# Attention through induced points and a two-layer network in one kernel: some steps of the first attention put at other visits, and a planner that links a late chain's parts and scores the last visit

## The chip, the cores and the metric

The kernel runs on one core of one Trainium2 chip. The metric is the device time of one execution in microseconds (us); of several executions the median is taken. A core has five engines that work side by side, each with its own instructions in order: TensorE (PE in the profile) multiplies matrices into PSUM, of which the kernel uses 8 banks of 128 x 512 fp32 numbers; ScalarE (ACT) computes functions such as exponentials and ReLUs and copies; VectorE (DVE) does element-wise work and reductions; GpSimd (POOL) does element-wise work on SBUF; SyncE (SP) issues DMAs here. An engine that needs another's result waits for a semaphore.

## The reference

Four batches of 12480 rows of 128 numbers pass two attentions and then a network with a parametric ReLU. Cut to what matters:

```python
def mab(q, kv):
    s = scale * (q @ kv.transpose(0, 2, 1))
    a = np.exp(s - s.max(-1, keepdims=True))
    a /= a.sum(-1, keepdims=True) + 1e-09
    return a @ kv
h = mab(I, x)          # 32 induced points look at all rows of a batch
x = mab(x, h)          # each row looks at the 32 results
h = x @ w_in           # 128 -> 2048
g = np.maximum(h, 0.0) + alpha * np.minimum(h, 0.0)
out = g @ w_out        # 2048 -> 128
```

## The kernel before

**Folding.** A row's second attention is a product of its 32 weights (`a2`) with the 32 results of its batch, and `w_in` follows at once; so the kernel forms `HW` = results x `w_in` once a batch, and a row's hidden numbers are its weights times `HW`. The parametric ReLU is split in two: alpha times the hidden number, which is linear and goes through `HA` (32 x 128) in `linear`, and (1 - alpha) times a plain ReLU, with 1 - alpha inside `W1`.

**Visits.** The loop at the end runs over blocks of 512 rows, four visits a block (`visits`), 390 visits in all; the last two blocks, made of rows that are left over, take 4 and 2. In a visit TensorE computes four banks `hh` of hidden numbers (`visit`, L848), then the second product of the visit before (`second`, L874, 16 products that add up in the bank `bp`). Between the two, each of the four `hh` is turned into a bf16 tile `gt` by a ReLU, on ScalarE (L861) or VectorE (L863). Each fourth visit a block's sum is copied out of PSUM and stored (`finish`, L927 or L929, store L934), and every eighth visit two blocks' linear parts are computed (L901).

**Steps between the visits.** What prepares later blocks is put behind a visit's products by hand: `at(n, fn, ...)` files a step under visit n (`todo`), and the loop runs a visit's steps in the order in which they were filed. There are two kinds.

- For each group of 2048 rows (16 visits, first visit n): the second scores (`b_scores`) are copied out of PSUM, their maximum is taken (`b_max`, VectorE), subtracted (`b_less_pool`, GpSimd), the exponential taken (`b_exp`, ScalarE, the step that stands as a lambda), summed (`b_sum`, GpSimd), inverted (`b_rec`, VectorE), multiplied into four copies (`b_mul`, GpSimd) and transposed by a DMA (`b_turn`) into `a2`. The list `when` gives their visits.
- For each piece of the next batch (six of 2048 rows with eight visits between them, and a short one of 192 rows, number 1): load, cast (GpSimd), a transposing DMA (`a_turn`), scores against the induced points with their running minimum (`a_scores_least`, at the visit `score`), exponential (`a_exp`, ScalarE, at `look`), the factor that rescales older sums (`a_fac`, ScalarE), a transposing DMA of the exponentials (`a_e1`, one visit behind `look`), and the product with the rows, added up (`a_h_add`, at `join`). At a batch's end `a_max`, `a_factors`, `a_parts`, `a_den` and `a_sum` close the sums and `a_w_both` and `a_lin` form `HW` and `HA`.

All DMAs of this phase are issued by SP, in the order of the program.

**The planner.** Before the loop records anything, `Plan.choose` searches over all visits with a beam of 64 states. For each visit it chooses which of the four ReLUs go to ScalarE ("a") and VectorE ("v"), which engine copies an output, and for each step's chain of work (its `cost`, a list of engine and ns) whether it runs at once ("n") or late ("l"), that is behind the second ReLU of the next visit (`run_waiting`). `Plan.step` advances modelled times of TensorE, ScalarE, VectorE and the PSUM banks for one visit. A state's score is TensorE's modelled time plus a part of what the other engines lag behind. The best path decides the engines, the order and the banks of the built kernel; nothing is decided while it runs.

Of the kernel before, what the change touches and what calls it, by code (L numbers as in the profile page):

```python
# [30 lines left out]
def kernel(  # L31
# [82 lines left out]
    class Plan:  # L114
# [41 lines left out]
        def step(self, state, n, relus, ways):  # L156


            pe, a, v, e1, free, held, late = state
            cols, linear, accs, last, chains = self.visits[n]  # L160
            busy = {"a": a, "v": v}
            free, held, used = list(free), dict(held), []

            def take(pe):
                k = min(range(BANKS), key=lambda k: max(free[k] + self.SEM, pe))
                used.append(k)
                pe = max(pe, free[k] + self.SEM)
                free[k] = self.NEVER
                return pe, k

            hh, mine = [], []
            for r in range(R):
                k = min(range(BANKS), key=lambda k: free[k])
                used.append(k)
                mine.append(k)
                pe = max(pe, free[k] + self.SEM) + 4
                free[k] = self.NEVER
                hh.append(pe + cols * 0.417 + self.ARRIVE)
            out = []
            for r in range(R):  # L180
                if r == 2:
                    for k, ns, ready, bank in late:
                        busy[k] = max(busy[k], ready) + ns
                        if bank is not None:
                            free[bank] = busy[k] + 100
                lat, per, over = self.RELU[relus[r]]
                out.append(max(busy[relus[r]], hh[r]) + lat + per * cols)
                free[mine[r]] = out[r]
                busy[relus[r]] = out[r] - over
            pe += cols * 0.417  # L190
            for k in accs[0]:
                if k not in held:
                    pe, held[k] = take(pe)
            pe += linear + self.MODE
            for k in accs[1]:
                if k not in held:
                    pe, held[k] = take(pe)
            for r in range(R):
                pe = max(pe, e1[r] + self.SEM) + last * self.FREE
            waits = []  # L200
            for chain, way in zip(chains, ways):
                ready, bank = 0, None
                for kind, ns in chain:
                    if kind == "!":
                        continue
                    if kind == "free":
                        free[ns] = ready + 100
                        continue
                    if kind == "acc":
                        ready, bank = pe + self.ARRIVE, held.pop(ns)  # L210
                        continue
                    if kind in "ps":
                        if kind == "s":
                            pe, bank = take(pe)
                        pe += ns
                        ready = pe + self.ARRIVE
                        continue
                    k = way[0] if kind == "f" else kind
                    ns = self.COPY[k] if kind == "f" else ns
                    if way[-1:] == "l":  # L220
                        waits.append((k, ns, ready, bank))
                    else:
                        busy[k] = ready = max(busy[k], ready) + ns
                        if bank is not None:
                            free[bank] = ready + 100
                    bank = None
                if bank is not None:
                    free[bank] = ready + 600
            new = pe + self.MODE, busy["a"], busy["v"], tuple(out), tuple(free)
            return (*new, tuple(held.items()), tuple(waits)), used  # L230

        def choose(self):
            start = tuple(430.0 if k == BANKS - 1 else 0.0 for k in range(BANKS))
            beam = [((0.0, 0.0, 330.0, (0.0,) * R, start, (), ()), None)]
            relus = ["".join(w) for w in product("av", repeat=R) if 0 < w.count("a") < R]
            for n, (*_, chains) in enumerate(self.visits):
                ways = []
                for chain in chains:
                    kinds = [k for k, _ in chain]
                    if "f" in kinds:  # L240
                        ways.append([e + w for e in "av" for w in "nl"])
                    elif "!" in kinds or not {"a", "v"} & set(kinds):
                        ways.append([""])
                    else:
                        ways.append(["n", "l"])
                found = {}
                for state, path in beam:
                    for way in product(*ways):
                        for relu in relus:
                            new, used = self.step(state, n, relu, way)  # L250
                            at = new[0] + 390
                            over = max(new[1] - at, 0) + max(new[2] - at, 0)
                            over += sum(w[1] for w in new[6]) * 0.3
                            score = new[0] + 0.3 * over
                            ends = sorted(max(x - new[0], -200) for x in new[4])
                            key = (
                                *(int(x - new[0]) // 16 for x in new[1:3] + new[3]),
                                *(int(x) // 16 for x in ends if x < self.NEVER / 2),
                                new[6],
                            )  # L260
                            if key not in found or score < found[key][0]:
                                found[key] = (score, new, (path, relu + "".join(way), used))
                best = sorted(found.values(), key=lambda f: f[0])[: self.WIDTH]
                beam = [(new, path) for _, new, path in best]
            path, taken, banks = beam[0][1], [], []
            while path:
                path, these, used = path
                taken.append(these)
                banks.append(used)
            self.taken = iter("".join(reversed(taken)))  # L270
            self.banks = iter([k for used in reversed(banks) for k in used])

    plan = Plan()
# [972 lines left out]
    def at(n, fn, *args, cost=()):  # L1246


        todo.setdefault(max(n, 0), []).append((fn, args, cost))
# [11 lines left out]

    for b, s, nt in groups[1:]:
        n = first[b, s]
        when = [n - 23, n - 19, n - 16, n - 14, n - 13, n - 11, n - 9, n - 6]
        if (b, s) == (0, 1):
            when = [0, 2, 3, 6, 7, 9, 9, 9]
        if (b, s) == (0, 2):
# [32 lines left out]
    for b in range(B - 1):  # L1300
# [3 lines left out]
        for p, pc in enumerate(whole_pieces):  # L1304
            m = n + (8 * (p - 1 + (not b and p > 2)) if p > 1 else p)
            load, cast, turn = m - 3, m + 6, m + 8
            score = m + 15 if p > 1 else n + 16
            look = score + 1 + (p == 1)
            join = m + (24 if p == whole_pieces[-1].k else 23) if p > 1 else n + (31 if p else 23)
            if not b:  # L1310
                load, cast, turn = {
                    0: (-1, -1, 6), 1: (-1, 9, 10), 2: (4, 9, 11)
                }.get(p, (load, cast, turn))
                score, look = (score, look) if p > 1 else (score + 4, look + 4)
                join = n + 31 if p < 2 else n + 39 if p < 3 else join
            f = pc.full
            if load >= 0:
                at(load, on, b + 1, a_load, pc)
# [12 lines left out]
                cost=[("s", 215 if f else 85), ("v", 800 if f else 460)],  # L1331
            )
            at(look, on, b + 1, a_exp, pc, cost=[("a", 717 if f else 430)])
            at(look + 2, on, b + 1, a_fac, pc, cost=[("a", 220)] if p else [])
            at(look + 1, on, b + 1, a_e1, pc)
            small_at(
                join, on, b + 1, a_h_add, pc, cost=[("s", 226 if f else 115), ("v", 260)]
# [13 lines left out]
    for n, (blk, i) in enumerate(visits):  # L1351
        before = visits[n - 1][0] if n else None
        nt = before.nt * before.per if n else 0
        chains = [cost for _, _, cost in todo.get(n, ()) if cost]
        if i == 0 and n > NV:
            copy = ("f", 0) if n > ST else ("v", 610)
            chains.insert(0, [("acc", before.k), copy])
            if n == 2 * NV:
                chains.insert(0, [("acc", 0), copy])
        both = [b.k for b in pairs.get(n, ())]  # L1360
        cost = nt * Plan.FREE if both else 0
        plan.visits.append(
            (blk.nt * blk.per * P, cost, (both, [before.k] if n else []), nt, chains)
        )
    plan.choose()

    prev = None
# [49 lines left out]
```

## Time and profile before

| | |
|---|---|
| median of 3 runs | 591.48 us (591.35 to 591.55) |
| the profiled execution | 593.02 us |
| its span, first to last instruction | 591.1 us, granted clock 1.0 |
| DMA, packets' time as a share of 16 engines, main queue | 56.0% |
| VectorE, ReLUs (L863) | 706 of 683 ns mean |
| a load of 1 MB (`xs`), issue to landing, median | 6.4 us |
| transposing DMA of a piece (`xT`), median | 6.6 us |
| transposing DMA of a group's weights (`a`), median | 4.7 us |
| transposing DMA of exponentials (`e`), median | 3.0 us |

The profile is of one execution, taken by the hardware profiler. "L874" is line 874 of the kernel. A group's row gives its line, engine, operation, tiles (written <- read), shapes and count, then the busy time in us and the mean ns of one, then the idle time of the engine just before. The chain of waits follows the work that ended last back from the last instruction; its pieces are listed as start, length, engine, tile and line. The timeline lists start, length, engine, line, operation, tiles and count; a bracket tells how long the engine had stood before and what ended it. For a DMA the length in SP's timeline is that of its issue; the time to landing stands in the DMA view.

### The profile page before, as it was taken

To read this page: it belongs to the slowest core of one execution; us is meant where nothing else is said; L and a number is where in the kernel's file an instruction comes from. 1 tells how busy PE (TensorE), PEld (TensorE's weight loads), DVE (VectorE), ACT (ScalarE), POOL (GpSimd) and SP (SyncE) were. 2 spreads that over 40 slices of the span, in tenths; PEclk is the share of its full clock that TensorE was granted. 3 is DMA by queue.
4 is the path that set the end of the run, shared out by engine and by line. 5 is a ranking of instruction groups with operands and counts; after the bars stand their busy time and mean duration, and the time that the engine had idled before them with its cause. 6 is when DMAs were issued, how large, how long until landed. Compare 5 with 4: busy or idle time off the path is not lost.

```text
span 591.1 us, 23015 instructions
## 1 busy us (share of the span) xinstructions
PE 580.7 (98%) x9443; PEld 436.2 (74%) x9443; DVE 534.4 (90%) x974; ACT 536.8 (91%) x1085; POOL 217.2 (37%) x259
## 2 busy tenths in 40 slices
PE   7899999999999999999999999999999999999997
PEld 3577777777777777777777777777777777777776
DVE  5799999988998998999999899999999999999996
ACT  5699999999999999999998999999999998999986
POOL 3575552523325426313226256124034134144110
PEclk9999999999999999999999999999999999999999
DMA  8786799734188899432256999741331331441321
GB/s 334 252 213 169 153 256 217 116 91 74 38 240 185 184 205 222 103 82 70 77 151 176 216 216 221 143 99 38 92 75 54 91 81 48 118 85 58 91 69 48
DMA packets 121964, 80.56 MB, mean 136 GB/s; under 512 B 103761, under 2 KB 105729, under 8 KB 118785
## 3 DMA queue, kind: packets, MB, share of 16 engines
q1 hardware_dynamic: 121632, 78.99, 56.0%
q8 instruction: 74, 1.21, 0.8%
q14 instruction: 34, 0.27, 0.1%
q10 hardware_dynamic: 224, 0.09, 0.1%
HBM read 28.07 MB, written 25.56 MB: 91 GB/s over the span
## 4 chain that ended last, share of the span: by engine, by line
PE 94%; DMA 3%; POOL 1%; DVE 0%; ACT 0%; issue 0%; DVEq 0%; SPq 0%; POOLq 0%
PE bp L874 66%; PE hh L848 22%; DMA xs<-in_x_dram 3%; PE bp L901 2%; PE hh L684 2%; PE hh L498 1%; PE hh L378 1%; POOL xn L348 0%; PE bp L1000 0%; PE hh L638 0%; DVEq L1412 0%; PE hh L607 0%; PE hh L622 0%; PE hh L1033 0%; PE hh L819 0%
## 5 line engine op out<-in xcount | busy, mean ns | idle before, releaser
L861 ACT ACTIVATE gt<-hh 128x512 bf16<-128x512 f32 x854 | 455.2, 606 | 34.3 <-PE hh L848 29.4
L863 DVE TENSOR_SCALAR gt<-hh 128x512 bf16<-128x512 f32 x706 | 453.4, 683 | 24.5 <-PE hh L848 13.2
L874 PE MATMUL bp<-W,gt 128*128 128x128 bf16 x6240 | 417.2, 220 | 0.7 <-DVE gt L863 0.7
L874 PEld LDWEIGHTS <-gt 128*128 128x128 bf16 x6240 | 349.3, 98 | 85.0 <-issue 76.5
L848 PE MATMUL hh<-a,HW 32*128 32x512 bf16 (+2 forms) x1664 | 156.0, 370 | 0.5 <-DVE a L827 0.5
L798 POOL TENSOR_TENSOR rep<-e,rc 128x2048 bf16<-128x2048 f32 (+2 forms) x26 | 84.8, 3265 | 23.0 <-DVE rc L789 22.6
L766 POOL TENSOR_TENSOR e<-e,smx 128x512 f32<-128x512 f32 (+1 forms) x24 | 24.6, 1027 | 154.6 <-ACT gt L861 79.4
L848 PEld LDWEIGHTS <-HW 32*128 32x128 bf16 x1664 | 40.4, 91 | 42.0 <-issue 5.9
L752 POOL TENSOR_TENSOR t<-e 128x256 f32<-128x256 f32 (+1 forms) x24 | 17.2, 718 | 144.1 <-ACT e L728 144.1
L927 ACT COPY ob<-bp 128x512 f32<-128x512 f32 (+1 forms) x63 | 36.9, 586 | 4.6 <-PE bp L874 1.7
L752 POOL TENSOR_TENSOR t<-t 128x128 f32<-128x128 f32 (+3 forms) x100 | 30.5, 305 | 7.8
L331 POOL CAST xn<-xs 128x2048 bf16<-128x2048 f32 x17 | 32.1, 1891 | 1.3 <-DMA xs<-in_x_dram 0.7
L929 DVE COPY ob<-bp 128x512 f32<-128x512 f32 x31 | 21.2, 684 | 5.2 <-PE bp L874 5.2
L417 DVE TENSOR_SCALAR_CACHE_REDUCE s<-hh 128x512 f32<-128x512 f32 (+2 forms) x29 | 17.9, 619 | 2.2 <-PE hh L378 1.9
L901 PEld LDWEIGHTS <-a 32*128 32x128 bf16 x392 | 14.9, 93 | 5.8 <-issue 0.2
L901 PE MATMUL bp<-HA,a 32*128 32x128 bf16 x392 | 19.1, 214 | 0.0
L443 ACT ACTIVATE e1T<-s,rm 128x512 bf16<-128x512 f32 (+1 forms) x25 | 17.9, 718 | 1.1 <-DVE rm L427 1.0
L761 DVE TENSOR_REDUCE smx<-e 128x16 f32<-128x512 f32 (+1 forms) x24 | 15.9, 661 | 0.0
L728 ACT ACTIVATE e<-e 128x512 f32<-128x512 f32 (+1 forms) x24 | 15.0, 624 | 0.0
L742 ACT COPY e<-hh 128x512 f32<-128x512 f32 (+1 forms) x22 | 13.4, 610 | 0.0
L684 PE MATMUL hh<-hT,xT 128*128 128x32 bf16 x372 | 13.0, 176 | 0.0
L523 DVE SCALAR_TENSOR_TENSOR hs<-hs,fac,hh 128x128 f32<-128x128 f32 (+1 forms) x21 | 7.2, 344 | 6.0 <-PE hh L498 5.3
(117 smaller groups left out, 195.2 us busy)
## 6 DMA issues: line engine op xcount, KB each, us to landing
out_dram<-ob SPq DMA_DIRECT2D x97, 256.0 KB, 2.5
xs<-in_x_dram SPq DMA_DIRECT2D x23, 1024.0 KB, 6.4
xs<-in_x_dram SPq DMA_DIRECT2D x2, 512.0 KB, 8.4
w_in_f<-in_moe_w_in_dram SPq DMA_DIRECT2D x1, 1024.0 KB, 9.9
a<-rep SPq DMA_TRANSPOSE x27, 4.7
xs_left<-in_x_dram SPq DMA_DIRECT2D x4, 96.0 KB, 5.8
xT<-xn SPq DMA_TRANSPOSE x18, 6.6
e<-e1T SPq DMA_TRANSPOSE x18, 3.0
```

What stands on the lines that cost most here:

```text
L331: nc.gpsimd.tensor_copy(out=st.xn[s][:], in_=xs[:])
L684: nc.tensor.matmul(ps[w, t, :], st.xT[:, tile0[s] + t, w], hTs[b][:], start=True, stop=True)
L752: nc.gpsimd.tensor_tensor(out=t[:, :n], in0=src[:, :n, :w], in1=src[:, :n, w : 2 * w], op=ADD)
L766: nc.gpsimd.tensor_tensor(out=st.e2[s][:, :n], in0=st.e2[s][:, :n], in1=st.m2[s][:, :n].unsqueeze(2).broadcast_to([P, n, M]), op=SUB,)
L798: nc.gpsimd.tensor_tensor(out=st.rep[s][:, ts], in0=st.e2[s][:, ts].unsqueeze(2).broadcast_to([P, n, R, M]), in1=rc[:, ts].unsqueeze(2).un ...
L848: nc.tensor.matmul(hh[:, q * cols + w.start : q * cols + w.stop], HWs[b][rows, v * P : (v + 1) * P], a2[rows, t0 : t0 + nt, :].rearrange(" ...
L861: nc.scalar.activation(out=gt[:, :cols], in_=hh[:, :cols], func=RELU)
L863: nc.vector.tensor_relu(gt[:, :cols], hh[:, :cols])
L874: nc.tensor.matmul(blk.acc[:, t * C : (t + 1) * C], gt[:, (q * nt + t) * P : (q * nt + t + 1) * P], W1[:, k, :], start=(not blk.begun), st ...
L901: nc.tensor.matmul(blk.acc[w, t * C : (t + 1) * C], blk.a2[rows, blk.t0 + t, w], HAs[b][rows, :], start=(not blk.begun and t == 0), stop=F ...
L927: nc.scalar.copy(out=ob[:, :nt], in_=acc)
L929: nc.vector.tensor_copy(out=ob[:, :nt], in_=acc)
```

## The change

Four things are changed; no instruction is added or removed.

```diff
             for r in range(R):
                 if r == 2:
-                    for k, ns, ready, bank in late:
-                        busy[k] = max(busy[k], ready) + ns
+                    done = 0
+                    for k, ns, ready, bank, linked in late:
+                        done = max(busy[k], ready, done if linked else 0) + ns
+                        busy[k] = done
                         if bank is not None:
                             free[bank] = busy[k] + 100
...
-                ready, bank = 0, None
+                ready, bank, linked = 0, None, False
...
                     if way[-1:] == "l":
-                        waits.append((k, ns, ready, bank))
+                        waits.append((k, ns, ready, bank, linked))
+                        linked = True
...
                             score = new[0] + 0.3 * over
+                            if n == len(self.visits) - 1:
+                                score = new[0] - self.MODE
+                                for ready in new[3]:
+                                    score = max(score, ready + self.SEM) + self.end * self.FREE
...
-        when = [n - 23, n - 19, n - 16, n - 14, n - 13, n - 11, n - 9, n - 6]
+        when = [n - 23, n - 20, n - 16, n - 13, n - 12, n - 10, n - 9, n - 6]
...
             score = m + 15 if p > 1 else n + 16
-            look = score + 1 + (p == 1)
+            look = score + 3 + 3 * (p == 1)
...
+            if p == 1 and b:
+                score, look = score + 4, look + 4
...
-            at(look + 2, on, b + 1, a_fac, pc, cost=[("a", 220)] if p else [])
+            at(look + 3, on, b + 1, a_fac, pc, cost=[("a", 220)] if p else [])
             at(look + 1, on, b + 1, a_e1, pc)
...
+    plan.end = visits[-1][0].nt * visits[-1][0].per
     plan.choose()
```

- In the planner's model a late chain's second part now begins only when its first part is done; before, the parts of a late chain could overlap.
- In the last visit a state is scored by the modelled end of the last second product, which waits for each ReLU in turn, instead of the end of the visit.
- In each group but the first two the maximum is filed one visit earlier, and the exponential, the sum and the reciprocal one visit later each.
- A whole piece's exponential is filed two visits later, the short piece's four visits later against its scores, and these scores, from batch 2 on, four visits later themselves. The transposing DMA of the exponentials moves with the exponential, the factor by one visit more. The products that use them stay where they were.

The planner's choices follow from these: the engines of ReLUs and copies and what is late change from visit 12 on.

## The prediction

> **What bounds the kernel now.** First the page: its busy shares and its chain of waits.
>
> ```profile
> span 591.1 us, 23015 instructions
> PE 580.7 (98%) x9443; PEld 436.2 (74%) x9443; DVE 534.4 (90%) x974; ACT 536.8 (91%) x1085; POOL 217.2 (37%) x259
> PE bp L874 66%; PE hh L848 22%; DMA xs<-in_x_dram 3%; PE bp L901 2%; PE hh L684 2%; PE hh L498 1%; PE hh L378 1%; POOL xn L348 0%; PE bp L1000 0%; PE hh L638 0%; DVEq L1412 0%; PE hh L607 0%; PE hh L622 0%; PE hh L1033 0%; PE hh L819 0%
> ```
>
> TensorE is the bound, and the change takes no matmul from it. So the only thing to win is time in which TensorE stands. To find that time I read the chain of waits piece by piece. An undisturbed visit is two pieces, 0.33 us for the first products and 1.00 us for the second; a longer piece holds a wait.
>
> ```profile
> 403.64 0.33 PE hh L848 x4
> 403.97 1.00 PE bp L874 x16
> ```
>
> From visit 0 (30.5 us) to the end of the full blocks (577 us) I find 27 such pieces, and one wait that shows itself as other engines' work. Each excess below is the row less 0.33 or 1.00.
>
> ```profile
> 30.51 0.40 PE hh L848 x4
> ...
> 101.60 0.45 PE hh L848 x4
> ...
> 196.50 0.55 PE hh L848 x4
> ...
> 241.17 0.46 PE hh L848 x4
> ...
> 378.85 0.46 PE hh L848 x4
> ```
>
> By stretch the excesses add up to 0.74 us up to 130 us (batch 1 is being prepared), 1.29 us from 164 to 263 us (batch 2), 0.70 us from 302 to 401 us (batch 3), and none that counts in the visits between, which prepare nothing. The largest wait stands by itself; the first fence is the chain, the second the timeline of TensorE's weight loads where it ends:
>
> ```profile
> 131.63 0.59 ACT gt L861
> 132.22 0.20 ACT ex L577
> ...
> 132.44 0.18 DVE dx L587
> ...
> 132.80 0.61 DVE gt L863
> ```
>
> ```profile
> 133.45 0.45 PEld L874 LDWEIGHTS <-gt 128*128 128x128 bf16 x8 [0.67 <-DVE gt L863]
> ```
>
> Here `a_parts` of batch 1 was put off (a late chain) into a visit where ScalarE has three ReLUs. VectorE reaches `dx`, which needs ScalarE's `ex`, and stands; the ReLU behind `dx` comes late, and TensorE's second product with it. 0.67 us is lost. One more wait, 0.37 us, stands in the very last second product:
>
> ```profile
> 585.05 1.29 DVE L863 TENSOR_SCALAR gt<-hh 128x512 bf16<-128x512 f32 x2 [0.43 <-PE hh L848]
> 585.10 1.09 ACT L861 ACTIVATE gt<-hh 128x512 bf16<-128x512 f32 x2
> 586.39 0.67 PEld L874 LDWEIGHTS <-gt 128*128 128x128 bf16 x12 [0.37 <-DVE gt L863]
> ```
>
> All that can be won is 0.74 + 0.67 + 1.29 + 0.70 + 0.37 = 3.8 us, or 0.6%.
>
> **The linked chain** (planner). The two parts of `a_parts`, and those of `a_factors`, are now costed one after the other. In the changed plan `a_parts` of batch 1 is still late, in visit 69, but the ReLUs of that visit go to VectorE first and ScalarE last, so nothing on VectorE stands behind `dx` in that visit, and ScalarE has no ReLU of the visit ahead of `ex`, only one copy (0.59 us, below). I take the 0.67 us as won. The least is 0.4 us: the copy's 0.59 us may still push ScalarE's two ReLUs back by the part of it that exceeds the 0.3 us or so a visit leaves ScalarE over.
>
> **Exponentials two visits later, short piece apart.** What the change spreads is seen where a piece's scores are taken:
>
> ```profile
> 238.62 0.68 DVE L417 TENSOR_SCALAR_CACHE_REDUCE s<-hh 128x512 f32<-128x512 f32 x1
> 239.42 3.07 DVE L863 TENSOR_SCALAR gt<-hh 128x512 bf16<-128x512 f32 x5
> 239.90 0.72 ACT L443 ACTIVATE e1T<-s,rm 128x512 bf16<-128x512 f32 x1
> ```
>
> VectorE spends 0.8 us on the scores (238.62 to 239.42), and at once ScalarE spends 0.72 us on the exponential. VectorE then runs five ReLUs without a pause, and the next first product but one waits 0.13 us (241.17 above). The waits at 101.6 and 378.9 us have the same place, and others too: one to three visits behind scores. In the changed plan ScalarE takes three ReLUs in the visit after the scores, and VectorE more of them where the exponential stands. The wait at 196.5 us and its like in batch 3 follow the visit where the whole and the short piece are scored together; now they are four visits apart. So the cause of most of the 0.74 + 1.29 + 0.70 us goes. Up to visit 11 the plan is the same and keeps its 0.15 us. I take 2/3 of the rest, 1.7 us, as won, before what follows; ends: 0 and 2.6 us.
>
> **What the moved step issues.** Each exponential is followed by a transposing DMA of `e1`, also two visits later, while the product that needs it (`a_h`, L498) stays. On SP's queue it is moved past an output's store, and, for every other whole piece, past `b_turn`, the transposing DMA of a group's weights. SP takes its instructions in order, and landings in the trace follow that order. The fourth piece of batch 2, in the timeline of SP:
>
> ```profile
> 225.86 4.10 SPq L355 DMA_TRANSPOSE xT<-xn  x1
> 230.42 1.71 SPq L474 DMA_TRANSPOSE e<-e1T  x1
> 232.23 0.53 SPq L934 DMA_DIRECT2D out_dram<-ob  x1
> 232.86 2.33 SPq L806 DMA_TRANSPOSE a<-rep  x1
> ```
>
> The DMA view restricted to this `e1` and this `b_turn` gives issue to landing, and TensorE's timeline the product's start:
>
> ```profile
> e<-e1T SPq DMA_TRANSPOSE x1, 3.9
> a<-rep SPq DMA_TRANSPOSE x1, 5.8
> 237.90 0.29 PE L498 MATMUL hh<-xn,e 128*32 128x128 bf16 x8
> ```
>
> Before, `e1` landed at 230.42 + 3.9 = 234.3, 3.6 us ahead of its product, and `b_turn` at 238.7. Behind `b_turn` it lands some 0.5 us after that (it moves a quarter of what `b_turn` moves, and that takes 2.33 us to issue), 239.2: 1.3 us late if `b_turn` stays where it is. But `b_turn` no longer has `e1` (1.71 us of issue) ahead of it. The group's exponential is one visit later, its GpSimd sum with it, and the piece's cast stands behind that sum, so `a_turn` (225.86) and `b_mul`, which forms the weights, move back by up to one visit, 1.33 us; `a_turn` then ends its issue near 231.3, and `b_turn` can follow a store behind it, near 231.5 to 231.9. That is 1.0 to 1.4 us earlier than now, and `e1` lands from 237.8 to 238.2: at its product, not before. So I cost it at 0 to 0.3 us against the old clock, but TensorE cannot come earlier than that here: what batch 2 had won up to this product is given back, about half of its 1.29 us. In batch 3 the same rows are earlier:
>
> ```profile
> 370.50 2.65 SPq L806 DMA_TRANSPOSE a<-rep  x1
> a<-rep SPq DMA_TRANSPOSE x1, 4.6
> 375.58 0.41 PE L498 MATMUL hh<-xn,e 128*32 128x128 bf16 x16
> ```
>
> 370.5 + 4.6 + 0.5 = 375.6 with `b_turn` unmoved, and 1 us less with it earlier: no wait there. I take 0.6 us as given back in all.
>
> The Trainium skill bears on this in DMA: Bandwidth & Descriptors, section "Latency and other measured facts": a transposing DMA moves 261 GB/s. By that the 128x2048 bf16 of `b_turn` (0.52 MB) would take an estimated 2.0 us instead of the 5.8 us from issue to landing seen here; `e1` behind it would land near 234, and nothing would be given back: 0.6 us less, still inside the forecast's own range. The trace speaks against it.
>
> **Group steps by one visit.** The group's maximum one visit earlier, its exponential, sum and reciprocal one later; `b_mul` and `b_turn` stay. GpSimd is busy 37% and covers it; if it didn't, the first products of the next group would wait for `b_turn`, which in batch 3 lands at 375.1, in visit 238 of a group whose first visit is 240, so more than a visit is spare. Cost 0.
>
> **Engines.** Comparing the programs' orders, 8 ReLUs go from ScalarE to VectorE, and 12 output copies the other way.
>
> ```profile
> L861 ACT ACTIVATE gt<-hh 128x512 bf16<-128x512 f32 x854 | 455.2, 606 | 34.3 <-PE hh L848 29.4
> L927 ACT COPY ob<-bp 128x512 f32<-128x512 f32 (+1 forms) x63 | 36.9, 586 | 4.6 <-PE bp L874 1.7
> ```
>
> ScalarE gets 12 x 0.586 - 8 x 0.533 (455.2/854) = 2.8 us more, VectorE about as much less. At 91% and 90% busy both lie under TensorE on the whole. In quiet visits the group's exponential and an output copy now stand in neighbouring visits of ScalarE, twelve times in the plan; I cost this at 0, since ScalarE is a visit ahead there, and keep up to 0.13 us each (one exponential, one copy and six ReLUs at 0.52 us are 4.3 us, the three visits 4.2 us), 1.6 us.
>
> **The last visit** is now scored to its end: ScalarE first, VectorE second. The second ReLU then ends at 585.10 + 1.09 = 586.19 instead of 585.05 + 1.29 = 586.34: 0.15 us won; ends 0 and 0.37.
>
> **The sum.** 0.67 + 1.7 - 0.6 + 0.15 = 1.9 us won. The profiled execution took 593.02 us, its span 591.1 and 1.9 around it, 1.5 us above the median of the runs (591.48); it becomes 591.1. The median becomes 591.48 - 1.9 = 589.6 us. Its own range goes from 0.9 us won (0.4, half of the 1.1 us that the exponentials keep, nothing at the end) to 3.6 us (0.67 + 2.6 + 0.37, nothing given back): 587.9 to 590.6.
>
> **The rivals.** *The win is eaten.* TensorE gets no faster than its DMAs: everything won ahead of an `e1` product is given back there, and only what comes behind the last such product of a batch stays: the 0.67 us, 0.13 us twice or so, the end's 0.15 us, about 1.0 us; 590.5 us, and with small new waits 591. For it: the landings above; against it: batches 1 and 3 have room.
>
> *Slower: `e1` behind `b_turn`.* If `b_turn` does not move forward, `e1` lands late at the seven places (two or three a batch) where it follows on SP with four visits to its product. The price of each lies between 0.06 us (375.64 against 375.58) and 1.3 us (batch 2); at the middle, 0.7, seven cost 4.9 us, less the 1.0 us that stays won: +3.9 us, 595.4 us. It decides once `b_turn` of batch 2's fourth piece is issued later than some 231.9 us on the old clock. Against it: the room that `e1` leaves ahead of `b_turn`. The Trainium skill has the rule behind it in the same page, section "Queues, rings and completion order": each DMA engine consumes a ring's descriptors in ring order. The order of the landings agrees.
>
> *The plan's costs do not hold.* The new plan loses in quiet visits (1.6 us) about what it wins elsewhere: 591.2 us. Against it: the old plan, made with the same costs, has no wait there.
>
> **How the numbers follow.** Forecast 0.57, win eaten 0.18, slower 0.13, costs do not hold 0.12. 0.2% is 1.2 us, about what counts as a change. Faster by more than that (below 590.3): nine tenths of the forecast, a third of the eaten win and some of the last, 0.60. Slower (above 592.7): 0.13 and a part of the last, 0.16. Within: 0.24. The range goes from 587.9 to 592.4; outside remain the slower case and little else.
>
> **What would show it.** Right: no chain through `dx` near 132 us; no excess one to three visits behind scores; the last second product resumes near 586.2 less what was won. The `e1` step is wrong if L498 waits for a DMA; the chain then has a DMA piece `e<-e1T`, and `b_turn` lands just ahead. The quiet-visit cost is wrong if L848 or L874 pieces between 263 and 302 us, or beyond 401 us, exceed 0.33 and 1.00. The prediction falls if such waits add up to more than 0.7 us.

## The result, and the profile after

The changed kernel takes 593.16 us (median of 22 runs, 591.92 to 595.20), the kernel before 591.48 us (22 runs, 591.25 to 592.26). The ratio is 1.0028, 95% interval 1.0020 to 1.0035: slower by 1.7 us, where 1.9 us less was forecast. The runs also spread over 3.3 us, against 1.0 us before.

The profiled execution took 592.05 us, one of the shorter ones. Its page:

```profile
span 590.3 us, 22988 instructions
PE 579.8 (98%) x9443; PEld 436.3 (74%) x9443; DVE 532.8 (90%) x969; ACT 537.1 (91%) x1090; POOL 216.7 (37%) x259
PE bp L881 65%; PE hh L855 21%; PE bp L908 2%; DMA e<-e1T 2%; PE hh L691 2%; PE hh L505 1%; PE hh L385 1%; DMA xs<-in_x_dram 1%; PE hh L370 1%; PE bp L1007 1%; PE hh L488 0%; PE hh L645 0%; ACT gt L868 0%; PE hh L614 0%; PE hh L629 0%
```

Lines have moved by seven (L874 is now L881, L848 L855, L498 L505). The span is shorter than the 591.1 us of before, and that misleads. In the chain of waits the first visit begins here:

```profile
29.18 0.40 PE hh L855 x4
```

In the profile of before it began at 30.51, though both programs are the same up to there; in every later profile of these runs it lies between 28.4 and 29.3 us. The profiled execution of before had lost 1.3 us on its way to the first visit. From the first visit to the end it took 591.1 - 30.5 = 560.6 us; the changed kernel takes 590.3 - 29.2 = 561.1.

New in the chain is a DMA, `e<-e1T`. Who waits for it stands in the waits of TensorE's weight loads from 29 to 590 us (waiting instruction, releaser, us in total, times, longest):

```profile
PEld L505 <- DMA e<-e1T: 1.7, 3, 1.1
PEld L505 <- DMA e<-e1T_left: 1.2, 1, 1.2
```

Before there was no such row. 2.9 us in four waits, and the timeline of the weight loads has the places, visits 126, 142 and 222:

```profile
212.42 0.11 PEld L505 LDWEIGHTS <-e 128*32 128x32 bf16 x2 [1.18 <-DMA e<-e1T_left]
212.84 0.23 PEld L505 LDWEIGHTS <-e 128*32 128x32 bf16 x16 [0.31 <-DMA e<-e1T]
...
236.29 0.23 PEld L505 LDWEIGHTS <-e 128*32 128x32 bf16 x16 [0.31 <-DMA e<-e1T]
...
351.40 0.23 PEld L505 LDWEIGHTS <-e 128*32 128x32 bf16 x16 [1.11 <-DMA e<-e1T]
```

The two long ones are where the short and the second whole piece of batches 2 and 3 are joined. SP's timeline ahead of the first, and the DMA view of the three transposes in it:

```profile
205.95 2.33 SPq L813 DMA_TRANSPOSE a<-rep  x1
208.37 1.34 SPq L481 DMA_TRANSPOSE e<-e1T_left  x1
209.76 1.75 SPq L481 DMA_TRANSPOSE e<-e1T  x1
```

```profile
a<-rep SPq DMA_TRANSPOSE x1, 6.1
e<-e1T_left SPq DMA_TRANSPOSE x1, 4.0
e<-e1T SPq DMA_TRANSPOSE x1, 3.0
```

`b_turn` lands at 205.95 + 6.1 = 212.1, the two `e1` right behind it at 212.4 and 212.8, and at these times L505 starts. SP spends 5.4 us on issuing the three. The chain shows the stop from TensorE's side: its products end at 209.1, and nothing of TensorE stands in it until 212.84.

```profile
208.75 0.36 PE hh L855 x4
209.12 0.59 ACT gt L868
209.71 0.05 issue
209.76 3.03 DMA e<-e1T
212.79 0.04 issue
212.84 0.41 PE hh L505 x16
```

(A chain names who released whom; TensorE itself worked on up to 211.4 us there and then stood for 1.0 us.)

### The profile page after: what moved, and what is told of

Same layout as the page of the kernel before. It is cut to its first block, busy times and chain, and to the rows that moved or that the text cites. A ratio compares the mean times of both kernels' runs of the same rounds, so it can differ in the third digit from the quotient of the medians.

```text
span 590.3 us, 22988 instructions
## 1 busy us (share of the span) xinstructions
PE 579.8 (98%) x9443; PEld 436.3 (74%) x9443; DVE 532.8 (90%) x969; ACT 537.1 (91%) x1090; POOL 216.7 (37%) x259
## 4 chain that ended last, share of the span: by engine, by line
PE 95%; DMA 3%; ACT 1%; DVE 0%; issue 0%; POOL 0%; SPq 0%; POOLq 0%
PE bp L881 65%; PE hh L855 21%; PE bp L908 2%; DMA e<-e1T 2%; PE hh L691 2%; PE hh L505 1%; PE hh L385 1%; DMA xs<-in_x_dram 1%; PE hh L370 1%; PE bp L1007 1%; PE hh L488 0%; PE hh L645 0%; ACT gt L868 0%; PE hh L614 0%; PE hh L629 0%
## 5 line engine op out<-in xcount | busy, mean ns | idle before, releaser
L870 DVE TENSOR_SCALAR gt<-hh 128x512 bf16<-128x512 f32 x714 | 458.7, 685 | 29.9 <-PE hh L855 18.2
L881 PE MATMUL bp<-W,gt 128*128 128x128 bf16 x6240 | 416.5, 220 | 0.0
L881 PEld LDWEIGHTS <-gt 128*128 128x128 bf16 x6240 | 349.4, 98 | 82.6 <-issue 74.1
L855 PE MATMUL hh<-a,HW 32*128 32x512 bf16 (+2 forms) x1664 | 154.5, 371 | 0.5 <-DVE a L834 0.5
L855 PEld LDWEIGHTS <-HW 32*128 32x128 bf16 x1664 | 40.2, 91 | 41.8 <-issue 5.8
L934 ACT COPY ob<-bp 128x512 f32<-128x512 f32 (+1 forms) x75 | 44.7, 596 | 1.0 <-PE bp L881 0.5
L936 DVE COPY ob<-bp 128x512 f32<-128x512 f32 x19 | 13.0, 684 | 0.0
```

What stands on the lines that cost most here:

```text
L855: nc.tensor.matmul(hh[:, q * cols + w.start : q * cols + w.stop], HWs[b][rows, v * P : (v + 1) * P], a2[rows, t0 : t0 + nt, :].rearrange(" ...
L870: nc.vector.tensor_relu(gt[:, :cols], hh[:, :cols])
L881: nc.tensor.matmul(blk.acc[:, t * C : (t + 1) * C], gt[:, (q * nt + t) * P : (q * nt + t + 1) * P], W1[:, k, :], start=(not blk.begun), st ...
L934: nc.scalar.copy(out=ob[:, :nt], in_=acc)
```

## The experiments

Two theories. **Q**: the loss is the queue: `e1` is issued behind `b_turn` and lands after its product could start. **P**: the planner's new engines, order and lateness cost the time.

### e1 ahead of b_turn, the plan unchanged

```diff
-        when = [n - 23, n - 20, n - 16, n - 13, n - 12, n - 10, n - 9, n - 6]
+        when = [n - 23, n - 20, n - 16, n - 13, n - 12, n - 10, n - 9, n - 5]
```

> The changed kernel, only b_turn filed one visit later, so that SP issues the e1 transposes ahead of it; b_turn has no cost in the planner, so the plan is the same. Theory Q (the loss is e1 landing late behind b_turn on SP's queue): the waits before L505 at visits 126, 142 and 222 (1.08 + 0.35, 0.20, 1.15 us in the changed kernel's profile) go, the time falls from 593.2 to about 590.3 us (589.6 to 591.0), and the spread of its runs from 3.3 us to about 1 us. Should b_turn then land after its group's first visit, L855 at visits 128 and 224 waits instead. Theory P (the new plan's engines and lateness cost the time): no change, 592.5 to 593.8 us.

590.24 us (589.34 to 591.78), ratio to before 0.9980, 0.9971 to 0.9989. Moving one step on SP's queue by one visit (`b_turn`, one DMA a group), with the same plan, takes 2.9 us from the changed kernel. The waits at 126, 142 and 222 are gone. The spread is 2.4 us, not 1: the profiled execution, the longest of the runs (591.78), has other late landings, and the one that the expectation named for `b_turn` at visit 128:

```profile
PEld L505 <- DMA e<-e1T: 2.0, 2, 1.1
PEld L855 <- DMA a<-rep: 0.7, 1, 0.7
```

The loss stays away although the plan is the same, so P is refuted as its cause; Q stands. But it doesn't cover every late `e1`: the two left in this profile are at visits 214 and 230, and no `b_turn` is issued just ahead of them.

### One part alone

Each is the kernel before with one part of the change's diff, and nothing else.

> The kernel before with the planner's two changes alone (linked late chains, last visit scored to its end). Q: the 0.67 us wait behind dx goes and some 0.15 us at the end, 590.7 us (590.3 to 591.3). P: the planner's choices are what loses, 592 us or more.

> The kernel before with the pieces' steps alone moved (exponentials, e1 transposes, factors, the short piece's scores). Q: the late e1 at visits 126 and 222 are there, waits of 1 us or more before L498, 592.5 us (591.8 to 594) and a spread of 2 us or more. P: no such waits, 590 to 591.3 us.

> The kernel before with the group steps alone moved (maximum one visit earlier; exponential, sum and reciprocal one later). Q: nothing on TensorE's path, 591.5 us (591.1 to 592). P: output copies and group exponentials stand in neighbouring visits, L848 or L874 pieces over 0.33 and 1.00 us between 263 and 302 us, 592.5 us or more.

| alone on the kernel before | median, us | runs from to | ratio to before, 95% |
|---|---|---|---|
| planner | 590.14 | 589.81 to 591.01 | 0.9972 to 0.9989 |
| pieces' steps | 593.27 | 592.41 to 595.09 | 1.0022 to 1.0051 |
| group steps | 593.91 | 593.65 to 594.28 | 1.0031 to 1.0056 |

The planner's part wins 1.2 us by itself, a little more than Q's range allowed; its profile has no wait behind `dx` and none for a DMA. The pieces' steps bring the late `e1` with them, more of it than the changed kernel's profile shows, in a longer execution (594.77 us); the waits of the weight loads:

```profile
PEld L498 <- DMA e<-e1T: 2.4, 3, 1.3
PEld L498 <- DMA e<-e1T_left: 1.3, 1, 1.3
```

These 3.7 us are not all that this execution lost there. TensorE's timeline at visit 126 and, behind it, the granted clock in stretches of 1 us (from and to, length, TensorE's busy time and matmuls, granted clock as a share of full speed, busy share and GB/s of the DMA engines):

```profile
212.69 0.29 PE L498 MATMUL hh<-xn_left,e 128*32 128x128 bf16 x2 [1.14 <-DMA e<-e1T_left]
214.12 0.41 PE L498 MATMUL hh<-xn,e 128*32 128x128 bf16 x16 [1.15 <-DMA e<-e1T]
...
215.01 1.50 PE L874 MATMUL bp<-W,gt 128*128 128x128 bf16 x16
...
216.98 1.89 PE L874 MATMUL bp<-W,gt 128*128 128x128 bf16 x16
```

```profile
215.00:216.00 1.00, 1.00 (x18) 0.73 0.60 213
216.00:217.00 1.00, 1.00 (x10) 0.50 1.04 369
217.00:218.00 1.00, 1.00 (x14) 0.50 0.96 313
218.00:219.00 1.00, 1.00 (x13) 0.56 0.96 335
```

Right behind two stops of 1.14 and 1.15 us the granted clock fell to half for about 3 us, and the second products took 1.50 and 1.89 us instead of the 1.07 us that this view gives an undisturbed one. From the drop in these four rows (0.27 + 0.50 + 0.50 + 0.44) that is an estimated 1.7 us at most on top of the waits. No other profile here has such a drop while TensorE works, also not those with single stops of 1.0 to 1.6 us or with two of 0.96 and 0.79 us.

The group steps lose 2.6 us alone, where Q had expected nothing, though not in the quiet visits that P had named. The wait behind `dx` of batch 1 now stands in all three batches, here in batch 2 (chain):

```profile
257.66 0.59 ACT gt L861
258.25 0.19 ACT ex L577
...
258.47 0.18 DVE dx L587
...
258.83 0.61 DVE gt L863
```

And at visit 126 VectorE has its hands full: sums, scores, running minimum, then two ReLUs, for the last of which TensorE waits 0.22 us. That place alone explains little, as the kernel before waits 0.17 us for VectorE in the same second product.

### Two parts, and the short piece

The first two take one part out of the changed kernel; the third leaves the short piece's exponential nearer to its scores:

```diff
             if p == 1 and b:
-                score, look = score + 4, look + 4
+                score, look = score + 4, look + 1
```

> The changed kernel with the pieces' steps put back (planner and group steps changed). Alone the group steps lost 2.6 us, with a wait behind dx in all three batches. If the unlinked model was the reason, the linked one takes these waits away: 590.2 us (589.5 to 590.8), no wait before L505. If the group steps cost by themselves (a copy and an exponential in neighbouring visits of ScalarE): 591.5 to 593 us.

> The changed kernel with the group steps put back (planner and pieces' steps changed). Q: e1 is as late as in the changed kernel, waits of 1 us or more before L505 at visits 126 and 222, 592.5 us (591.6 to 593.5), spread 2 us or more. P: 589.5 to 590.5 us, if the group steps were what cost the time.

> The changed kernel with the short piece's exponential three visits earlier in batches 2 and 3, so that at visits 122 and 218 one e1 instead of two stands behind b_turn. Q: the second piece's e1 is issued 1.2 to 1.3 us earlier but still lands behind b_turn; the wait at visit 126 falls from 1.4 to some 1.0 us, at 222 from 1.15 to some 0.3 us; 592.3 us (591.5 to 593). If the pair were the whole cause: both waits gone, 590.3 us.

Planner and group steps: 591.58 us (ratio 0.9993 to 1.0011). The waits behind `dx` are gone, so the unlinked model was one reason for them; but 1.4 us over the planner alone stay. In its profile 0.5 us of that lie between visits 24 and 92 and 0.5 us between 92 and 160, as short waits at many places, the longest two at these first products (0.33 us undisturbed):

```profile
131.09 0.67 PE hh L855 x4
...
176.67 0.57 PE hh L855 x4
```

Why the moved group steps bring them isn't shown. Both guesses were half right. Planner and pieces' steps: 593.04 us (1.0022 to 1.0045), with 1.8 + 1.1 us of waits for `e1` in its profile: putting the group steps back changes nothing as long as `e1` is late. The short piece early: 590.71 us (589.80 to 591.85, ratio 0.9981 to 0.9997), better than expected of Q. The wait at 222 is gone and the stretch of batch 3 short; at 126 there is one wait still, for the second piece's `e1` alone:

```profile
PEld L505 <- DMA e<-e1T: 1.6, 1, 1.6
```

In the medians one `e1` fewer behind `b_turn` takes back 2.4 us of the changed kernel's loss, but the profile doesn't show so much. Batch 3 (visits 188 to 256) takes 98.1 us instead of 99.2; batch 2 (visits 92 to 160) takes 99.6 us as against 99.7, since its one wait is no shorter than the two of the changed kernel together (1.18 + 0.31). So the pair decides at visit 222; at 126 the order behind `b_turn` is enough. What else the medians gain is open.

### All exponentials one visit earlier

```diff
-            look = score + 3 + 3 * (p == 1)
+            look = score + 2 + 3 * (p == 1)
```

> The changed kernel with every exponential, and its e1 transpose, one visit earlier (two visits behind the scores instead of three; the short piece's too), so that SP issues e1 a visit ahead of b_turn, and b_turn stays where it is. Theory Q (queue order): no wait before L505 at visits 126, 142, 222, and none for b_turn at visit 128; the changed kernel without these waits: 589.3 us (588.7 to 590.2), spread about 1 us. Theory P (engines): the exponential is nearer to the scores again, ReLU waits of 0.1 to 0.2 us return at several places, 590.3 to 591.5 us.

590.55 us (589.91 to 591.00; ratio 0.9977 to 0.9995), outside Q's range and inside P's. `e1` is in time except once (0.6 us, at visit 230), and the spread is 1.1 us; but the stretches of batches 2 and 3 take 98.8 and 98.7 us, not the 98.1 of the changed kernel without its waits. In batch 3 the wait at 230, a place that Q had not named, makes up that difference. In batch 2 nothing waits for `e1`, and there TensorE's pieces are longer again at several places, by 0.23 us at most, as P had it: with the exponential nearer to the scores some of the gain goes.

### e1 ahead only where it was late

```diff
             if p == 1 and b:
-                score, look = score + 4, look + 4
+                score, look = score + 4, look + 1
+            if p in (2, 4):
+                look -= 1
```

> The changed kernel with e1 ahead of b_turn where that can be had by one visit: the short piece's exponential three visits earlier in batches 2 and 3, the second and fourth whole pieces' exponentials (numbers 2 and 4) one visit earlier. All else as changed. Theory Q (queue order): no wait before L505 of more than 0.1 us at visits 126, 142, 222; the stretch of batch 2 and that of batch 3 take 98.1 us each, as the changed kernel's do without these waits (99.69 - 1.63, 99.20 - 1.15); 589.4 us (588.9 to 590.1), below both kernels. If the ReLU waits come back with the earlier exponentials: 590 to 591 us.

> The same with the group steps put back. With e1's waits gone the group steps' own part shows: as planner_only against planner_when it would be 1.4 us less than e1_ahead, 588.5 us; if the group steps help once the exponentials stand later, it is slower than e1_ahead, 590 us or more.

590.74 us (0.9982 to 0.9999) and 592.07 us (1.0002 to 1.0023), not the 589.4 and 588.5 us that were expected. Batch 2 does as expected, 98.1 us. But in batch 1 the second piece's `e1` now goes ahead of the short piece's, which then stands behind two halves of `b_turn` and that other `e1`, and lands late at visit 30; and at 214 the first piece's `e1` is late:

```profile
PEld L505 <- DMA e<-e1T_left: 1.3, 1, 1.3
PEld L505 <- DMA e<-e1T: 0.7, 1, 0.7
```

With the old group steps these two waits are longer (1.8 and 1.3 us), so the 1.3 us between the two kernels says little about the group steps by themselves.

> The changed kernel itself, for a second profile. Q: the waits before L505 at visits 126 and 222 are there again, together with others they make up what the span is longer by than 588.0 us or so, and their sizes differ from the first profile's (1.43 and 1.15 us), since they hang on when the DMAs before them land. P: other waits, between matmuls of L881 or L855.

This second execution took 591.76 us, with 3.1 us of waits for `e1`: 1.31 + 0.31 us at visit 126, 0.16 at 142, but only 0.18 at 222, where Q had expected a long one again. A new one of 1.15 us stands at 214 instead, and it brings TensorE later to 222 (chain):

```profile
334.55 4.42 DMA e<-e1T
338.97 0.04 issue
339.01 0.41 PE hh L505 x16
```

This is the first whole piece, the one that has three visits from its `e1` to its product, not four, and no `b_turn` is issued just ahead of it. In both profiles it is issued some 3.4 us before its product could start; in the first it lands after 2.4 us, here after 4.4.

### A version that beats both kernels

As above, but in batches 2 and 3 alone and with the first whole piece:

```diff
-            if p in (2, 4):
+            if b and p in (0, 2, 4):
                 look -= 1
```

> The changed kernel with e1 ahead of b_turn in batches 2 and 3 alone (batch 1 as changed, where the variant e1_ahead made the short piece's e1 land 1.4 us late at visit 30): the short piece's exponential three visits earlier, those of whole pieces 0, 2 and 4 one visit earlier, so that e1 of the first piece, late by 0.6 to 1.0 us at visit 214 in three profiles, is early too. Theory Q: no wait before L505 of more than 0.1 us at visits 30, 126, 142, 214, 222; batch 1 as in the changed kernel (31.5, 46.4, 17.44 us), batches 2 and 3 some 98.1 us each; 588.8 us (588.4 to 589.5), below both kernels and below planner_only. If TensorE, once ahead, meets the next late DMA: 589.8 us or more, with new waits before L505 or at b_turn.

589.24 us, inside Q's range; ratio to before 0.9968, 0.9958 to 0.9979. Eleven of twelve runs lie between 588.76 and 589.49, one at 592.62, whose mean granted clock, 0.993, is the lowest of all runs. One wait for `e1` is left, in batch 1, and where the changed kernel stood at visit 126 the chain is whole:

```profile
PEld L505 <- DMA e<-e1T: 0.4, 1, 0.4
```

```profile
209.93 0.33 PE hh L855 x4
210.25 1.00 PE bp L881 x16
211.25 0.44 PE hh L505 x18
211.69 0.22 PE hh L385 x4
```

## Why the prediction was wrong

**What there was to win** was sized rightly. Read in the same way, the changed kernel's chain has pieces over 0.33 and 1.00 us that add up to 0.35 us in batch 1's stretch (0.74 before), 0.14 in batch 2's (1.29) and 0.19 in batch 3's (0.70): about 2.1 us won, where 1.7 was forecast. (Where the chain runs over a DMA, at three places of 2.5 to 4.5 us, it shows no such pieces.) **The linked chain** took the 0.67 us away: in visit 69 ScalarE does a copy, then `ex`, and VectorE's ReLUs stand ahead of `dx`, as worked out.

```profile
129.41 0.60 ACT L934 COPY ob<-bp 128x512 f32<-128x512 f32 x1
129.52 1.29 DVE L870 TENSOR_SCALAR gt<-hh 128x512 bf16<-128x512 f32 x2 [0.17 <-PE hh L855]
129.88 0.34 ACT L584 ACTIVATE ex<-rm 128x7 f32<-128x7 f32 x1
...
130.72 0.16 DVE L594 TENSOR_TENSOR dx<-ex,da 128x7 f32<-128x7 f32 x1
```

**The last visit** resumes 0.20 us late instead of 0.37: 0.17 us won, 0.15 forecast.

```profile
585.50 0.67 PEld L881 LDWEIGHTS <-gt 128*128 128x128 bf16 x12 [0.20 <-ACT gt L868]
```

**What the moved step issues** is the step that failed. It named the queue, SP's order, `b_turn` and the price, and then worked the landing out at one place, the fourth piece of batch 2, as 0 to 0.3 us late. That place is right: 0.2 to 0.3 us. `b_turn` even moved forward more than was worked out, to 229.31 us from 232.86, which is 2.2 us counted from the first visit, where 1.0 to 1.4 was forecast. But 0.6 us was taken as "given back in all" from it and from one place in batch 3. At visits 122 and 218 two `e1` stand behind `b_turn`, not one, since the short piece's exponential was moved to the second piece's visit; they cost 1.18 + 0.31 and 1.11 us, and the whole term is 2.9 us (3.1 in the second profile), where 0.6 was taken. The first piece's `e1`, with three visits of room, was not followed at all; it cost nothing in the first profile and 1.15 us in the second. "Batches 1 and 3 have room" held for the place shown and not for visit 222. Each `e1` should have been followed to its product, the ones moved by four and eight visits first.

2.1 + 0.67 + 0.17 won and 2.9 lost leave nothing; one piece at 526 us, absent before, adds 0.3, and the measured difference from the first visit on is 0.4 to 0.5 us. The medians differ by 1.7. The rest is in no profile of the changed kernel, as both took 1.1 to 1.4 us less than its median. That it comes from the same wait is supported by the runs, though not seen in one: the three kernels with a late pair spread over 2.7 to 3.3 us, and putting `b_turn` behind `e1` takes back the full 2.9 us. A longer execution of another kernel with the late pair, the pieces' steps alone, shows two ways to such a loss: 3.7 us of waits, and behind them the drop of the granted clock, a price that the prediction did not have. The changed kernel's two longest runs (595.15 and 595.20 us) have a mean granted clock of 0.996 and 0.997, the other twenty 0.998 to 1.0; so such a drop is possible in those two, and doesn't explain the median.

**The slower rival** had the right mechanism, the wrong place of decision (the fourth piece of batch 2) and a condition that was not needed: `b_turn` did move forward, ahead of visit 126 by 1.8 us (205.95 against 209.05, counted from the first visit), and `e1` was late all the same. 595.4 us was too far; the truth lay between it and a range that ended at 592.4. **The eaten win** described the profiled execution best: what was won came back as waits at `e1`.

**Group steps at cost 0**: alone they cost 2.6 us, and 1.4 with the linked planner. The `dx` waits are part of the first figure, as the linked planner takes them away; how the rest comes about is open. In the whole change this part doesn't show: with or without it the time is 593.2 or 593.0 us. **Quiet visits at cost 0** held: from 263 to 302 us and beyond 401 us no piece is longer, but for the one at 526 us.

The Trainium skill (DMA: Bandwidth & Descriptors, "Latency and other measured facts") gives 261 GB/s for a transposing DMA with a non-contiguous middle dimension; by it `b_turn`'s 0.52 MB would take an estimated 2.0 us, and here it took 6.1 us to land, which decides.

What stays open: what the median holds beyond the two profiles, why the first piece's `e1` is late at 214 in some executions and not in others, and the single run of 592.62 us of the best version, of which only the low granted clock is known.

## What to carry to other kernels

A step that is moved takes its DMA along: follow each such DMA in the issuing engine's order to the instruction that needs it, and at every place, since the tightest one (two behind one long transfer) decides. When a planner models only the compute engines, what it wins can be lost on a queue that it does not know. And compare profiled executions from the first common point on, with the median beside them: here the spans had the opposite sign of the medians.

## What the runs showed of the hardware

A transposing DMA held SP for long. At visit 122 it was 2.33 us for 128x2048, 1.34 us for the short piece and 1.75 us for 128x512, so the third of three could not even be issued before 3.8 us had gone by. Over the changed kernel's profile the last kind took 1.2 to 2.2 us to issue and 2.4 to 4.9 us to land.

Landings vary from one execution to the next: 2.4 or 4.4 us for the same `e1` at the same place. The three kernels with a late pair spread over 2.7 to 3.3 us, and those without any late `e1` in their profile over 0.6 to 1.2 us, but for one run of the kernel before that took 592.75 us. The spread doesn't tell surely, though: one kernel with 2.0 us of such waits in its profile (`e1` ahead only where it was late) spread over 1.2 us.

In one profile TensorE stood for 1.14 and 1.15 us with 0.29 us of products between, and the granted clock went down to 0.50 for about 3 us soon after it resumed.
